# Block 2's q and x turned by VectorE and transfers instead of by TensorE, in a fused attention and SwiGLU kernel

## The chip, the cores and the metric

The kernel runs on one core of a Trainium2 chip. The metric is device time in microseconds (us) of that core. The kernel before took 1032.19 us, the median of three runs (1030.74 to 1032.48). A profile of one execution (1033.15 us, span 1031.2 us) stands behind every line below.

Names used: TensorE (PE in the profile, its weight loads PEld), VectorE (DVE), ScalarE (ACT), GpSimd (POOL), SyncE (SP, which computes nothing here but issues most transfers). SPq and ACTq are the instruction streams in which SP and ScalarE issue transfers.

## The reference, cut to what matters

```python
kv  = einsum('bhsd,bhse->bhde', k, v)          # batch 8, heads 8, seq 576, head_dim 64
a   = einsum('bhsd,bhde->bhse', q, kv)
a   = a / sqrt(mean(a*a, -1) + 1e-6) * g_norm
x   = a.transpose(0,2,1,3).reshape(4608, 512)  # tokens x model
g   = x @ w_gate                               # 512 x 1536
out = (g * sigmoid(g) * (x @ w_val)) @ w_out   # 1536 x 512
```

All is float32 for the purposes of this text. There is no softmax: attention is linear, so per head only the 64x64 matrix kv is needed.

## The kernel before, in words

**Blocks.** The 4608 tokens are worked in nine blocks of 512 (`BLK`), numbered 0 to 8. A block's attention (class `Att`) is woven into the feed-forward part (class `Ffn`) of the block before it: while block n is multiplied, block n+1's q is turned, multiplied by kv, scaled and turned again into x, with the model dimension on the partitions.

**Matrix products.** Block 0 is multiplied plainly (`plain_up`). From block 1 on the products are done in seven instead of eight block products (a Strassen-Winograd scheme; `Quad`, with numbers p = 1 to 7). Block 1 does this in one level for the up-projection (`Up`), blocks from `DEEP` = 2 on in two levels (`Inner`). The two-level form needs sums of weight blocks, called leaves here. They are computed once, during block 1, on VectorE (`leaf_steps`), are sent to DRAM by SP (tiles `w`, the helper `send`, L821), and are streamed back as 256 KB tiles `t` in every block from 2 on (class `Stream`, L793, 17 tiles for each third of the up-projection, through nine buffers). The pieces of work of a step are handed on: `Ffn.make` takes leaf steps in between matrix products; those of the last two weight pairs (j = 4 and 5) are kept in `latest` and are taken in the down-projection of block 1, in a room of 21 blocks named `xi`.

**Turning q and x.** There are two ways. In the first, TensorE multiplies by the identity, 16 products of 128x128 for q (`turn_q`, L335) and 16 for x (`turn_x`, L402), and a copy brings the result out of PSUM. In the second, q is loaded in strips of 32 columns (`load_quarters`, L281, 32 small transfers for a block), VectorE turns it in 32x32 blocks (L329), and no TensorE work is needed. For x, `blocks_x` turns 32x32 blocks on VectorE (L412), `place_x` puts the blocks into their places by 16 transfers (L426, eight on SP's queue and eight on ScalarE's), and `gain_x` multiplies by the gain in place (L431). The constant `TURNED` = 3 says from which block the second way is used; block 1's q (not its x) uses the strips as well. Block 2 uses the first way for both.

**The down-projection** (`Ffn.down`) runs the seven products in the order 1, 5, 6, 7, 2, 4, 3, or 1, 6, 5, 7, 2, 4, 3 where the next block is of the second way. After some of them a step of the next block's attention is put in (`Att.steps`): for the second way the whole attention after p = 1, the placing transfers after 5, the gain and the Strassen sums (`sums`) after 2. For the first way: half the attention after p = 1, x's first half and the second half of the attention after 6, x's second half and the sums after 2. `turn_t` lets GpSimd make three differences of `wo` tiles for each of p = 5, 7 and 4.

**What sets the order.** The statements are reordered engine by engine by a scheduler, whose priorities follow the program, and `tc.issue_after(x)` puts what is recorded within it behind x. Each engine then runs its own list in order, and a queue issues its transfers in order. The transfers of all queues share eight semaphores in turn: each waits for the one eight before it. In the built kernel before, SP's list in the down-projection of block 1 is: 20 of block 3's 32 q transfers, two leaf sends, the other 12, three weight tiles of block 2, two leaf sends, six more weight tiles, the two stores of block 1's output.

Of the kernel before, what the change touches and what calls it, by code (L numbers as in the profile page):

```python
# [14 lines left out]
P = 128  # L15
# [3 lines left out]
def kernel(  # L19
# [50 lines left out]
    NB = NT // BLK  # L70
# [44 lines left out]
    def ring():  # L115

        return r_pool.tile([P, 4, BLK], F32, name="r")
# [75 lines left out]
    class Att:  # L193


        def __init__(self, n):
            self.n = n

            self.cut, half = divmod(n, 2)
            self.split = half * D  # L200
            self.ps, self.z = {}, None
            self.q, self.k, self.v, self.room = [], {}, {}, None
            self.halves = []
            self.quarters = n == 1 or n >= TURNED

        def parts(self, t):

# [210 lines left out]
        def place_x(self):  # L418
            src = self.turned.rearrange("p i (x c) -> p (i x) c", c=P)
            self.x = x_pool.tile([P, 7, 2, HB], F32, name="x")  # L420
            dst = self.x[:, 0:4].rearrange("p o k (t c) -> p (o k t) c", c=P)
            rows = [slice(32 * r, 32 * (r + 1)) for r in range(4)]
            for a in range(4):
                for b in range(4):
                    queue = nc.scalar if b % 2 else nc.sync
                    queue.dma_start(out=dst[rows[b], :, rows[a]], in_=src[rows[a], :, rows[b]])  # L426

        def gain_x(self):
            for i in range(2):
# [56 lines left out]
        def steps(self):  # L486


            def whole():
                self.product(0, (m_psum, a_psum))  # L490
                self.product(1, (m_psum, b_psum))
                self.root(0, 2)
                for i in range(2):
                    self.scale(i)
                self.halves.append(self.scaled)
                self.blocks_x()

            def end():
                self.gain_x()
                self.sums()  # L500

            if self.n >= TURNED:
                return {1: whole, 5: self.place_x, 2: end}

            def last():
                self.turn_x(1)
                if self.n:
                    self.sums()

            def middle():  # L510
                self.turn_x(0)
                self.half(1, (m_psum, b_psum))


            return {1: lambda: self.half(0, (m_psum, a_psum)), 6: middle, 2: last}
# [7 lines left out]

    DEEP = 2

    TURNED = 3

    class Quad:

# [41 lines left out]
    class Up(Quad):  # L571
# [51 lines left out]
        def multiply(self, p):  # L623
            super().multiply(p)
            ffn = self.ffn
            if ffn.n != DEEP - 1:
                return

            if p == 5:
                self.leaf_room = ring().rearrange("p f (s c) -> p (f s) c", c=P)  # L630
            if p in (5, 7, 4):
                at = 3 * (5, 7, 4).index(p)
                ffn.making.extend(leaf_steps(self.j, [(self.w[p].unsqueeze(1), (p,))], self.leaf_room[:, at:]))
            if p == 3:
                if ffn.leaf_room is None:
                    ffn.leaf_room = x_pool.tile([P, 3, 7, P], F32, name="xi").rearrange("p a b c -> p (a b) c")
                halves = lambda t: t[self.j].rearrange("p (o i) c -> p o i c", o=2)
                steps = leaf_steps(self.j, [(halves(wg), (1, 2)), (halves(wv), (6, 3))], ffn.leaf_room)
                if self.j < NP - 2:
                    ffn.later.extend(steps)  # L640
                else:
                    ffn.latest.append(steps)

# [169 lines left out]
    def leaf_steps(j, sources, room):  # L813


        d, f = divmod(j, 2)
        i = 0

        def send(leaf, count, src):
            at = LEAVES.index(leaf)  # L820
            tc.keep_in_program_order(nc.sync.dma_start(out=stream.dram[d][:, at : at + count, f], in_=src))  # L821

        for t, os in sources:
            n = len(os)
            t = t.rearrange("p o i (e c) -> p o i e c", e=2)
            b11, t2_, b22 = t[:, :, 0, 0], t[:, :, 0, 1], t[:, :, 1, 1]
            to = room[:, i : i + 3 * n].rearrange("p (o r) c -> p o r c", r=3)
            yield lambda b22=b22, t2_=t2_: sub(nc.vector, t2_, b22, t2_)
            yield lambda b11=b11, t2_=t2_: add(nc.vector, t2_, t2_, b11)
            yield lambda t=t, t2_=t2_, to=to, n=n: sub(  # L830
                nc.vector, to[:, :, 0:3:2], t[:, :, 1], t2_.unsqueeze(2).to_broadcast([P, n, 2, P])
            )
            if os[0] not in RESIDENT:
                yield lambda t=t, o=os[0]: send((o, 1), 4, t[:, 0].rearrange("p i e c -> p (i e) c"))
            yield lambda b11=b11, t2_=t2_, to=to: sub(nc.vector, to[:, :, 1], b11, t2_)
            yield lambda i=i, n=n, o=os[0]: send((o, 4), 3 * n, room[:, i : i + 3 * n])
            i += 3 * n
# [88 lines left out]
    class Ffn:  # L926
# [52 lines left out]
        def down(self, nxt):  # L979

            down = self.down_
            fill = nxt.steps() if nxt else {}
            for p in (1, 6, 5, 7, 2, 4, 3) if 5 in fill else (1, 5, 6, 7, 2, 4, 3):
                if p == 1:
                    down.turn_t(7, self.ended)
                if p == 6:
                    down.turn_t(4, nxt.halves[0] if nxt and nxt.n >= TURNED else None)

                with tc.issue_after(nxt.multiplied.ins) if self.n == 0 and p in (5, 6) else ExitStack():
                    down.multiply(p)  # L990
                self.make(12)
                if p == 5 and self.n == DEEP - 1:
                    for i in range(2):
                        self.loads(i)
                if p in fill:
                    fill[p]()
                if p in (1, 7) and self.latest:

                    with tc.issue_after(nxt.scaled.ins):
                        for step in self.latest.pop(0):  # L1000
                            step()
                if p == 1:

                    with tc.issue_after(nxt.q_turned.ins) if self.n == 0 else ExitStack():
                        down.turn_s3()
# [60 lines left out]
    for n in range(NB):  # L1066
        ffn = Ffn(n, blocks[n])
        nxt = blocks[n + 1] if n + 1 < NB else None
        if n == 0:

            with tc.issue_after(squared.ins), tc.issue_after(scaled.ins):
                weights(2)
            ffn.plain_up(0, (0,))
            copied = blocks[0].copied
            blocks[0].turn_x(1)
            for f in range(NF):
                with tc.issue_after(blocks[0].copied.ins if f else copied.ins):
                    weights(2 * (f + 2))
                ffn.plain_up(f) if f else ffn.plain_up(0, (1,))
            weights(len(pieces))  # L1080
            pairs = wo.rearrange("p (j e) d -> p e j d", e=2)
            t2(pairs[:, 0, :, HD:DM], pairs[:, 1, :, HD:DM], pairs[:, 0, :, 0:HD])
            nxt.room = x_pool.tile([P, 3, 7, P], F32, name="xi").rearrange("p a b c -> p (a b c)")

            with tc.issue_after(sent.ins):
                for i in range(2):
                    nxt.load_kv(i)
                for i in range(2):
                    nxt.load_q(i)
            ffn.plain_end()  # L1090
            for g in range(2):
                nxt.kv(g)
        else:

            def third():
                nxt.kv(0)
                nxt.load_kv(1)

            def two_thirds():
                nxt.kv(1)  # L1100
                if nxt.n < TURNED:
                    for i in range(2):
                        nxt.load_q(i)

            ffn.up({4: third, 8: two_thirds} if nxt else {})
        if nxt:
            nxt.turn()
        if 0 < n < NB - 2:
            blocks[n + 2].load_kv(0)
        if TURNED - 2 <= n < NB - 2:  # L1110
            ffn.loads = blocks[n + 2].load_q
            if n >= DEEP:
                for i in range(2):
                    ffn.loads(i)
        ffn.down(nxt)
        if n == 0:
            blocks[2].load_kv(0)

            with tc.issue_after(nxt.halves[0].ins):
                for j in range(NP):  # L1120
                    t2(wv[j][:, 0:2], wv[j][:, 2:4], wg[j][:, 0:2])
# [31 lines left out]
```

## Time and profile before

| what | value |
|---|---|
| time, median of 3 | 1032.19 us |
| span of the profile | 1031.2 us |
| TensorE busy | 1013.0 us (98%) |
| VectorE busy | 703.9 us (68%) |
| GpSimd busy | 371.6 us (36%) |
| ScalarE busy | 230.2 us (22%) |
| HBM read, written | 138.02 MB, 22.41 MB |
| down-projection of block 1 (first product to block 2's start) | 238.6 to 279.8 us |
| same of block 2 (to block 3's start) | about 347.4 to 388.0 us |

How to read it: a line of the timeline has the start in us from the span's beginning, the duration, the engine, the line of the kernel, the operation with its tiles (out<-in) and how many were merged (x16). A bracket at the end tells how long the engine stood idle before it and what ended the wait. In the chain that ended last, the columns are start, duration and what. DVE x L111 and the like are the helpers `add`, `sub` and `mul` (L111 to L113). Matrix instructions come in two passes for each product of the program, so 12 products show as x24.

### The profile page before, as it was taken

The page shows a single profiled execution, that of the slowest core. Times are in us where ns is not written, and L with a number is a line of the kernel's source. Part 1 is how long each engine was busy: PE and PEld are TensorE (multiplying, and loading weights), DVE is VectorE, ACT ScalarE, POOL GpSimd, SP SyncE. Part 2 cuts the span into 40 slices and gives each one's busy share as a digit, 9 for nine tenths or more (in the row PEclk, how much of TensorE's full clock was granted, in tenths as well). Part 3 has the DMA queues.
Part 4 walks back from the last instruction along what each step waited for, and adds up shares of the span by engine and source line. Part 5 has one row for each costly group of instructions (what it writes and reads, how often), then busy time and mean ns, then how long its engine had stood idle before and what let it go on. Part 6 is the DMA issues. An engine that isn't in the chain of part 4 may idle for free.

```text
span 1031.2 us, 21440 instructions
## 1 busy us (share of the span) xinstructions
PE 1013.0 (98%) x8570; PEld 903.5 (88%) x8570; DVE 703.9 (68%) x1185; ACT 230.2 (22%) x359; POOL 371.6 (36%) x280
## 2 busy tenths in 40 slices
PE   5999999999999999999999999999999999999998
PEld 4544688888899989998999899988999899989997
DVE  2999796997766855585657576674669466856661
ACT  2666111222211211221112122111212111211110
POOL 0000543444035612462156305630455136513670
PEclk9999999999999999999999999999999999999999
DMA  7689614783778456855686468736862666066611
GB/s 215 195 261 266 119 37 128 186 223 72 205 202 248 90 133 209 248 126 114 192 242 163 68 205 240 198 53 186 236 199 50 169 196 193 22 165 205 189 30 41
DMA packets 252403, 168.15 MB, mean 163 GB/s; under 512 B 129168, under 2 KB 220432, under 8 KB 252304
## 3 DMA queue, kind: packets, MB, share of 16 engines
q1 hardware_dynamic: 225808, 163.37, 57.9%
q10 hardware_dynamic: 26432, 3.41, 2.0%
q8 instruction: 68, 1.11, 0.5%
q14 instruction: 31, 0.25, 0.1%
q0 software_dynamic: 64, 0.00, 0.0%
HBM read 138.02 MB, written 22.41 MB: 156 GB/s over the span
## 4 chain that ended last, share of the span: by engine, by line
PE 83%; DVE 10%; DMA 4%; SPq 1%; ACT 1%; issue 1%; DVEq 0%; ACTq 0%
PE b L712 26%; PE b L549 20%; PE c L712 13%; PE c L549 10%; PE a L712 6%; PE a L549 5%; DVE r L153 2%; PE m L355 1%; PE m L314 1%; SPq L281 1%; DVE r L147 1%; DMA h<-in_v_dram 1%; DVE r L152 1%; DMA ld<-in_v_dram 1%; DVE xi L112 1%
## 5 line engine op out<-in xcount | busy, mean ns | idle before, releaser
L111 POOL TENSOR_TENSOR r<-r 128x256 f32<-128x256 f32 (+1 forms) x105 | 110.7, 1060 | 310.1 <-DVE r L111 204.4
L111 DVE TENSOR_TENSOR r<-b,r 128x512 f32<-128x512 f32 (+1 forms) x273 | 162.1, 606 | 64.2 <-PE b L712 59.1
L112 POOL TENSOR_TENSOR t<-wo 128x512 f32<-128x512 f32 x81 | 117.1, 1470 | 191.6 <-DVE wo L111 106.9
L111 DVE TENSOR_TENSOR r<-c,r 128x512 f32<-128x512 f32 (+1 forms) x179 | 108.5, 618 | 95.0 <-PE c L712 55.5
L712 PE MATMUL b<-x,t 128*128 128x128 f32 x1092 | 151.0, 275 | 0.0
L712 PEld LDWEIGHTS b<-x,t 128*128 128x128 f32 x1092 | 136.5, 192 | 0.6
L111 DVE TENSOR_TENSOR r<-a,r 128x512 f32<-128x512 f32 (+1 forms) x99 | 62.5, 631 | 108.7 <-PE a L549 63.0
L712 PE MATMUL c<-xi,t 128*128 128x128 f32 x840 | 112.2, 275 | 0.4 <-DVE xi L111 0.4
L113 POOL TENSOR_TENSOR h<-r 128x1024 f32<-128x1024 f32 (+1 forms) x40 | 82.1, 2067 | 80.6 <-DVE r L111 72.8
L712 PEld LDWEIGHTS c<-xi,t 128*128 128x128 f32 x840 | 102.8, 192 | 0.5 <-DVE xi L111 0.5
L549 PE MATMUL b<-wo,h 128*128 128x256 f32 x432 | 99.5, 382 | 0.1
L549 PE MATMUL b<-t,h 128*128 128x256 f32 x432 | 96.9, 381 | 0.0
L549 PEld LDWEIGHTS b<-t,h 128*128 128x128 f32 x432 | 81.3, 190 | 11.3 <-issue 0.2
L549 PEld LDWEIGHTS b<-wo,h 128*128 128x128 f32 x432 | 79.9, 190 | 12.8 <-DVE h L113 2.5
L726 ACT COPY r<-b 128x512 f32<-128x512 f32 x63 | 36.9, 585 | 211.7 <-PE b L712 199.8
L712 PE MATMUL b<-xi,t 128*128 128x128 f32 x588 | 79.7, 276 | 0.0
L712 PEld LDWEIGHTS b<-xi,t 128*128 128x128 f32 x588 | 72.4, 192 | 0.0
L712 PE MATMUL b<-x,wg 128*128 128x128 f32 x336 | 52.7, 279 | 0.2 <-DVE x L112 0.2
L712 PE MATMUL b<-x,wv 128*128 128x128 f32 x336 | 51.3, 275 | 0.0
L549 PE MATMUL c<-t,s 128*128 128x256 f32 x216 | 48.3, 380 | 0.0
L549 PE MATMUL a<-wo,h 128*128 128x256 f32 x216 | 48.3, 379 | 0.0
L549 PE MATMUL c<-wo,h 128*128 128x256 f32 x216 | 48.1, 379 | 0.0
(131 smaller groups left out, 1579.8 us busy)
## 6 DMA issues: line engine op xcount, KB each, us to landing
t<-w SPq DMA_DIRECT2D x336, 256.0 KB, 3.6
out_dram<-r SPq DMA_DIRECT2D x17, 512.0 KB, 3.1
ld<-in_k_dram SPq DMA_DIRECT2D x26, 288.0 KB, 5.1
ld<-in_v_dram SPq DMA_DIRECT2D x26, 288.0 KB, 5.7
ld<-in_moe_w_gate_dram SPq DMA_DIRECT2D x12, 512.0 KB, 4.6
ld<-in_moe_w_val_dram SPq DMA_DIRECT2D x12, 512.0 KB, 4.4
ld<-in_moe_w_out_dram SPq DMA_DIRECT2D x12, 512.0 KB, 5.3
w<-t SPq DMA_DIRECT2D x18, 256.0 KB, 2.5
```

The lines of the kernel that those rows point to most:

```text
L111: add = lambda e, o, a, b: e.tensor_tensor(out=o, in0=a, in1=b, op=OP.add)
L112: sub = lambda e, o, a, b: e.tensor_tensor(out=o, in0=a, in1=b, op=OP.subtract)
L113: mul = lambda e, o, a, b: e.tensor_tensor(out=o, in0=a, in1=b, op=OP.mult)
L147: nc.vector.tensor_scalar(out=mag.bitcast(F32), in0=mag.bitcast(F32), scalar1=self.LOW, scalar2=self.HIGH, op0=OP.max, op1=OP.min,)
L152: nc.vector.tensor_scalar(out=sign, in0=high, scalar1=0x80000000, scalar2=None, op0=OP.bitwise_and)
L153: return nc.vector.scalar_tensor_tensor(out=mag, in0=mag, scalar=3, in1=sign, op0=OP.logical_shift_left, op1=OP.bitwise_xor)
L281: nc.sync.dma_start(out=to[32 * r : 32 * (r + 1), j, g0:g1], in_=q[b, 4 * i + 2 * j + h, s0 : s0 + 32 * (g1 - g0), 32 * d : 32 * (d + 1)]. ...
L314: nc.tensor.matmul(self.kv_ps[r][u * D : (u + 1) * D, g, :], lhsT=k[:, u, c, :], rhs=v[:, u, c, :], start=(c == 0), stop=(c == KT - 1),)
L355: self.multiplied = nc.tensor.matmul(self.ps[i][u][p : p + D, t, j, :], lhsT=self.qt[rows, 2 * i + t, j, p : p + D], rhs=kvs[b % 3][rows, ...
L549: nc.tensor.matmul(banks[e][:, e], lhsT=lhsT, rhs=rhs, start=first and i == 0 and (e == 0 or banks[0] is not banks[1]), stop=i == self.ste ...
L712: nc.tensor.matmul(ps[:, i, f], lhsT=self.weight(o, p, f), rhs=self.operand(o, p), start=first and (i, f) == (0, 0), stop=True, skip_group ...
L726: nc.scalar.copy(out=dst, in_=ps)
```

## The change

Block 2 goes over to the second way for both q and x, by `TURNED` = 2. Then the 32 products that turn them fall away from TensorE. Since the leaves of the last two weight pairs are still being made in that down-projection, they are moved: they now stand after p = 5 and p = 7, behind the scaling of block 2's attention and behind the last placing transfer of SP's queue (`nxt.placed`, a new name for it). Pair 5 gets a room of its own from the ring of work tiles instead of the second use of `xi`. The loads of block 3's q (`self.loads`) are put behind the same two marks. Which function builds the leaves' steps is now decided when their room is known (`steps` became a function of the room).

```diff
-            self.quarters = n == 1 or n >= TURNED
+            self.quarters = n > 0
...
-                    queue.dma_start(out=dst[rows[b], :, rows[a]], in_=src[rows[a], :, rows[b]])
+                    placed = queue.dma_start(out=dst[rows[b], :, rows[a]], in_=src[rows[a], :, rows[b]])
+                    if b % 2 == 0:
+                        self.placed = placed
...
-    TURNED = 3
+    TURNED = 2
...
-                steps = leaf_steps(self.j, [(halves(wg), (1, 2)), (halves(wv), (6, 3))], ffn.leaf_room)
+                steps = lambda room: leaf_steps(self.j, [(halves(wg), (1, 2)), (halves(wv), (6, 3))], room)
                 if self.j < NP - 2:
-                    ffn.later.extend(steps)
+                    ffn.later.extend(steps(ffn.leaf_room))
...
-                if p == 5 and self.n == DEEP - 1:
-                    for i in range(2):
-                        self.loads(i)
                 if p in fill:
                     fill[p]()
-                if p in (1, 7) and self.latest:
-
-                    with tc.issue_after(nxt.scaled.ins):
-                        for step in self.latest.pop(0):
+                if p in (5, 7) and self.n == DEEP - 1:
+
+                    with tc.issue_after(nxt.scaled.ins), tc.issue_after(nxt.placed.ins):
+                        room = self.leaf_room if p == 5 else ring().rearrange("p f (s c) -> p (f s) c", c=P)
+                        for step in self.latest.pop(0)(room):
                             step()
+                        if p == 5:
+                            for i in range(2):
+                                self.loads(i)
```

## The prediction

> **What bounds the kernel now.** I read the busy times first, then the chain that ended last, then the SP queue (which issues most transfers) around the place that the change touches: the down-projection of block 1, in which block 2's attention is worked out.
>
> ```profile
> PE 1013.0 (98%) x8570; PEld 903.5 (88%) x8570; DVE 703.9 (68%) x1185; ACT 230.2 (22%) x359; POOL 371.6 (36%) x280
> PE 83%; DVE 10%; DMA 4%; SPq 1%; ACT 1%; issue 1%; DVEq 0%; ACTq 0%
> ```
>
> TensorE is busy for 98% of the span and is 83% of the chain. Whatever leaves TensorE is won, as long as no other engine or transfer then comes too late for it. The chain in order of time shows what the change removes (columns: start, duration, what):
>
> ```profile
> 233.24 0.44 PE m L335 x4
> 233.67 0.22 PE b L335 x2
> ...
> 237.69 0.22 PE b L335 x2
> 237.91 0.44 PE m L335 x4
> 238.35 0.44 PE b L335 x4
> ...
> 255.62 0.87 PE m L402 x8
> ...
> 268.59 0.87 PE m L402 x8
> ...
> 279.82 0.89 PE b L712 x8
> ```
>
> L335 turns block 2's q, L402 its x; at 279.82 block 2's up-projection begins, with no pause before it. The SP queue in the same stretch:
>
> ```profile
> 238.73 10.36 SPq L281 DMA_DIRECT2D ld<-in_q_dram  x20
> ...
> 257.38 6.72 SPq L281 DMA_DIRECT2D ld<-in_q_dram  x12
> 264.21 1.40 SPq L793 DMA_DIRECT2D t<-w  x3
> ...
> 268.13 6.91 SPq L793 DMA_DIRECT2D t<-w  x6
> 275.29 5.68 SPq L936 DMA_DIRECT2D out_dram<-r  x2
> ```
>
> Block 3's q (L281) is asked for first, and then the first nine weight tiles of block 2 (L793). All nine are issued by 275.0, almost 5 us before block 2 starts. That is the slack which the change uses up. Block 2's own down-projection already does for block 3 what the change now does for block 2, so it has the prices:
>
> ```profile
> 344.15 17.80 SPq L281 DMA_DIRECT2D ld<-in_q_dram  x32
> 367.11 7.84 SPq L426 DMA_DIRECT2D x<-r  x8
> 375.07 3.44 SPq L793 DMA_DIRECT2D t<-w  x6
> ```
>
> There q goes out first, then x's placing transfers (L426), then the weight tiles. Last, one place where weight tiles are asked for late, at the start of block 6:
>
> ```profile
> 706.88 0.41 SPq L936 DMA_DIRECT2D out_dram<-r  x1
> 707.40 4.96 SPq L793 DMA_DIRECT2D t<-w  x9
> ```
> ```profile
> 713.82 0.71 PE L712 MATMUL a<-x,t 128*128 128x128 f32 x4 [0.79 <-DMA t<-w]
> ```
>
> The third of those tiles is released to TensorE at 713.77 in the chain, 6.9 us after the queue began this run with a store: 1.31 MB moved (0.52 of the store, three tiles of 0.26).
>
> [...] block 3's x needs two turns of 128x1024 (2.36 us together) and then 16 placing transfers. [...] So what stands behind a waiting transfer in SP's queue waits too; the trace agrees, SP issued nothing for 5.09 us at L426, waiting for VectorE. [...]
>
> **The change, part by part.**
>
> *Removed from TensorE.* q's turning takes 0.76 us at 233.24 to 234.00 and 1.10 us at 237.69 to 238.79: 1.86. x's takes 2 x 0.87 = 1.74. The two products (L355) stand apart now, 243.97 to 245.06 and 256.49 to 258.03, 2.63 us; block 3's in one piece took 353.84 to 355.86, 2.0 us: 0.6 less. Sum 4.2 us.
>
> *q in 32-wide quarters.* 32 small transfers in place of 4, at 0.53 us each on SP (17.0 to 17.8 us for 32 in all blocks), during block 1's up-projection, between the sends of weight leaves (L821). In the built order 16 of them come in a row behind the send that now starts at 213.4, so the sends that started at 215.2 move to about 222. Who waits: the leaf steps on VectorE that need their room again. VectorE meets the next such wait at about 227.7 (the instructions ahead of it summed), when the send of 222.9 should have landed (its median is 3.9 us). Bounds: 0, or up to 3 us if it lands late and TensorE then waits for VectorE. I take 0: both turns of q (2 x 1.23 against a copy of 0.69) fall at 230 to 233, where VectorE had 1.0 and 0.55 us idle.
>
> *x by VectorE and transfers.* Block 2's down-projection shows it: products at 353.84, x's transfers from 367.1 (13.3 us later), gain at 377.3, sums from 379.8, block 3 begins at 387.97 without a wait. Block 1 adds the leaves of the last two weight pairs to VectorE. Most fall into its 9.84 us idle before 376.89; the last 2.06 us stand ahead of x's sums. The sums TensorE needs third would be done some 2 us before their need. I price this at 0; at most 2 us.
>
> *The order on SP, the main point.* In the built order of the changed kernel SP has: two weight tiles, x's 8 transfers, two leaf sends, block 3's 32 q transfers, two more leaf sends, the store of block 1, and only then weight tiles three to nine. The waits on x's transfers and scaling were meant for the leaves, but q's loads stand behind the same ones, and the tiles behind q. Worked out:
> - Products start at 243.97 - 1.86, about 242.0. x's transfers from 242.0 + 13.2 = 255.2.
> - Eight of them on SP: 7.84 us in block 2, 5.76 in block 5; I take 7.4: 262.6.
> - Two leaf sends of 384 KB: 1.4 (1.32 and 1.76 before): 264.0. 32 q transfers: 17.4: 281.4.
> - The rest from block 6: 6.9 us for 1.31 MB. Here two sends, the store and tile three are 1.57 MB; the further 0.26 MB at about 290 GB/s (the rate of the stretch 215 to 225) adds 0.9. The tile lands at about 289.1; the tile behind costs TensorE 0.3 more: 289.4.
>
> When did the kernel before have as much done? The built order puts 20 of block 2's matrix products (two passes of 0.112 us each: 4.5 us) and 36 small k-v products (1.2 us) ahead of the first use of tile three: 279.8 + 4.5 + 1.2 = 285.5. From there both have the same work left. So the change costs 289.4 - 285.5 = 3.9 us. TensorE would arrive at about 281.3 and stand idle for near 8 us: the 4.2 us won are lost, and as much again. Later tiles follow at 0.9 us each, while TensorE takes some 1.4 us per tile (17 in a third of the up-projection, 23.3 us), so no second wait. 1032.2 + 3.9 = 1036.1; I say 1036.
>
> **Rivals.**
> - *All is hidden, faster.* If tile three landed by 281, only the 4.2 us of TensorE would count: 1028. For it: in blocks 2 to 7 the same scheme runs with no idle TensorE. Against: there q is loaded before x's transfers, and SP cannot bring 17 us of q, 7 of x and the sends between 255 and 281.
> - *Near balance.* Shorter x transfers (5.8), quick sends and a tile 5 us after its issue give a landing of about 286: 1032.5, no change that can be measured.
> - *More waits than one.* Leaf rooms late in the up-projection hold VectorE, by up to 3 us; SP's whole series then starts later by as much, so it adds fully: 1039. With slow transfers of x and q and longer landings: up to 1042.
>
> **How the numbers follow.** The late tile as worked out (1034.3 to 1039): 0.58. More waits (above): 0.17. Balance (1030.2 to 1034.2): 0.17. All hidden: 0.08. So slower 0.75, same 0.17, faster 0.08. SP's terms can err by 2 us down (x's transfers 1.6, sends 0.4) and by 3 up, and the waits of the up-projection only lengthen: 1031.5 to 1042 leaves out the hidden case and a little on both ends.
>
> **What would show it.** Right: SP shows L281 x32 between about 264 and 282, the tiles after it, and TensorE idle some 8 us before a use of t near 281 to 289, released by a DMA. L335 falls to the turns of block 0 and L402 to blocks 0 and 1. The start of block 2 at 275 to 276 confirms the gain. Wrong: block 2 entered later than 277 (x or VectorE is the bound), idle TensorE in 210 to 240 (leaf rooms), or the tiles issued before 278.

## The result, and the profile after

The changed kernel takes 1036.13 us, the median of four runs (1035.91 to 1037.1); the kernel before 1031.71 us in its four (1030.74 to 1032.48). The ratio is 1.0045, with a 95% interval of 1.0028 to 1.0063: slower by 4.4 us.

Busy times and the engines' shares of the chain, from the page of the changed kernel:

```profile
PE 1011.2 (98%) x8538; PEld 902.1 (87%) x8538; DVE 703.8 (68%) x1177; ACT 228.4 (22%) x354; POOL 371.4 (36%) x280
PE 87%; DVE 6%; DMA 3%; SPq 2%; issue 1%; ACT 1%; ACTq 0%; DVEq 0%
```

TensorE has 32 instructions fewer, 8538 against 8570 (a turning product is one pass, not two), and is busy for 1.8 us less, in a span that is 3.2 us longer. The queue of SP in the down-projection of block 1, in the timeline:

```profile
252.44 6.43 SPq L426 DMA_DIRECT2D x<-r  x8
259.89 0.97 SPq L823 DMA_DIRECT2D w<-xi  x2
261.00 18.37 SPq L281 DMA_DIRECT2D ld<-in_q_dram  x32
279.46 0.99 SPq L823 DMA_DIRECT2D w<-r  x2
280.55 1.64 SPq L938 DMA_DIRECT2D out_dram<-r  x1
282.29 4.37 SPq L795 DMA_DIRECT2D t<-w  x7
```

All 32 of block 3's q transfers (L281) now stand between x's placing transfers (L426) and all but the first two weight tiles of block 2 (L795). Tile three is the first of those seven, issued at 282.29. On TensorE, in the timeline:

```profile
263.33 0.79 PE L314 MATMUL m<-ld 64*64 64x64 f32 x34
...
269.34 5.34 PE L551 MATMUL c<-wo,h 128*128 128x256 f32 x24
274.52 0.61 PE L714 MATMUL b<-x,wg 128*128 128x128 f32 x4
...
279.18 0.81 PE L314 MATMUL m<-ld 64*64 64x64 f32 x38
286.65 1.23 PE L714 MATMUL a<-x,t 128*128 128x128 f32 x4 [6.67 <-DMA t<-w]
287.67 1.91 PE L714 MATMUL b<-xi,t 128*128 128x128 f32 x8
289.38 2.39 PE L714 MATMUL c<-xi,t 128*128 128x128 f32 x12
```

Block 2 begins at 274.52. TensorE then runs out at 279.98 and stands for 6.67 us until tile three lands. The chain, in order of time, holds the same transfer:

```profile
280.55 1.64 SPq L938
...
282.29 4.32 DMA t<-w
286.61 0.04 issue
286.65 1.23 PE a L714 x4
```

One thing more is to be seen in the timeline: the products behind the stop are slow. Eight products `b<-xi,t` take 1.91 us here, and 1.06 in the next use at 294.28. A table of stretches shows why (columns: stretch, its length, busy time of the five engines, granted TensorE clock, share of the DMA engines, GB/s):

```profile
283.00:284.00 1.00, 0.00 (x0) 0.00 (x0) 0.00 (x0) 0.00 (x0) 0.00 (x0) 1.00 1.05 376
284.00:284.50 0.50, 0.00 (x0) 0.00 (x0) 0.00 (x0) 0.00 (x0) 0.00 (x0) 0.90 1.07 279
284.50:285.00 0.50, 0.00 (x0) 0.00 (x0) 0.00 (x0) 0.00 (x0) 0.00 (x0) 0.50 0.93 209
...
290.50:291.00 0.50, 0.50 (x4) 0.50 (x4) 0.00 (x0) 0.00 (x0) 0.00 (x0) 0.50 0.99 381
291.00:291.50 0.50, 0.50 (x6) 0.50 (x5) 0.17 (x1) 0.00 (x0) 0.00 (x0) 0.77 1.06 410
```

The granted clock falls from 1.00 to 0.50 while TensorE stands and returns after it goes on. A mean of 0.90 over 284.0 to 284.5 puts the fall at 284.40, a mean of 0.77 over 291.0 to 291.5 the return at 291.23. From 286.65 to 291.23 TensorE worked at a granted clock of 0.50: 4.58 us for 2.3 us of work, as I estimate it (4.58 x 0.50). The 24 passes from 286.65 on took 4.95 us in all, against 2.68 before.

**The sum of it.** Two marks split the span: the product of block 1's up-projection after the one wait for VectorE, and the start of block 2. In the timeline of TensorE, before:

```profile
213.98 1.99 PE L549 MATMUL c<-x,wv 128*128 128x256 f32 x8 [0.74 <-DVE r L111]
...
279.66 0.61 PE L712 MATMUL b<-x,wg 128*128 128x128 f32 x4
```

After (block 2's start, at 274.52, is shown above):

```profile
212.43 1.99 PE L551 MATMUL c<-x,wv 128*128 128x256 f32 x8 [0.71 <-DVE r L111]
```

(The chain counts a start from the end of the product before it, so it has 279.82 for 279.66.)

| stretch | before | after | difference |
|---|---|---|---|
| start to the first mark | 213.98 | 212.43 | -1.55 |
| first mark to block 2's start | 65.68 | 62.09 | -3.59 |
| block 2's start to the end | 751.54 | 759.88 | +8.34 |

The first row I put down to single executions: in the profile of before the first loads landed 0.7 us later and TensorE waited 0.46 us at 124.33, neither in code that the change touches, and the second wait comes back in the profile of an experiment (0.34 us). The other rows are the change: 4.75 us lost between the first mark and the end, against 4.4 us by the medians. Of the 8.34 us, 6.67 are the stop and 2.3 the slow products behind it; 0.7 of k-v products of block 3 (L314, 34 passes at 263.33), which now lie ahead of block 2, go off. That leaves less than 0.1.

### The profile page after: what moved, and what is told of

The parts are those of the page before. It is cut to its first block, busy times and chain, and to the rows that moved or that the text cites. A ratio compares the mean times of both kernels' runs of the same rounds, so it can differ in the third digit from the quotient of the medians.

```text
span 1034.4 us, 21411 instructions
## 1 busy us (share of the span) xinstructions
PE 1011.2 (98%) x8538; PEld 902.1 (87%) x8538; DVE 703.8 (68%) x1177; ACT 228.4 (22%) x354; POOL 371.4 (36%) x280
## 4 chain that ended last, share of the span: by engine, by line
PE 87%; DVE 6%; DMA 3%; SPq 2%; issue 1%; ACT 1%; ACTq 0%; DVEq 0%
PE b L714 25%; PE b L551 19%; PE c L714 12%; PE c L551 9%; PE a L714 6%; PE a L551 5%; PE b L1021 4%; PE c L1021 4%; SPq L281 2%; PE m L314 1%; PE m L355 1%; DVE xi L112 1%; DMA t<-w 1%; DMA h<-in_v_dram 1%; DVE r L112 1%
```

## The experiments

Each ratio is to the kernel before, run on the same chip; 95% intervals in brackets.

**1. q early.** The loads go back to where they stood before the change, outside the two marks.

```diff
                 self.make(12)
+                if p == 5 and self.n == DEEP - 1:
+                    for i in range(2):
+                        self.loads(i)
                 if p in fill:
...
-                        if p == 5:
-                            for i in range(2):
-                                self.loads(i)
```

> The changed kernel with block 3's q loads taken out of the two marks and put directly after the product p = 5, as before the change; the queue then has them ahead of x's transfers. Late tile (my theory): the 6.67 us in which TensorE stood before its use of tile three fall away, and some 0.7 us of slowed products after it; 1028.5 us (1027.5 to 1029.5), 0.997 of the kernel before. TensorE enters block 2 without a stop for t. Rival, the work moved to VectorE costs (two turns of q, of x, leaves behind x): the place of a load does not matter to it, 1036. Rival, the bytes ahead of tile three (two sends, a store) and not the queue: the same bytes stand ahead of it here, so it stays at 1034 to 1036. Rival, x late: x's transfers now queue behind q, so x comes later and it gets worse, over 1037.

Measured: 1029.62 us, 0.9979 (0.997 to 0.9988). The stop for t is gone, and the VectorE and bytes rivals fall with it. It is 1 us short of the 1028.5 expected, and the trace shows where (queue of SP, then TensorE):

```profile
238.17 22.02 SPq L281 DMA_DIRECT2D ld<-in_q_dram  x32
260.30 6.07 SPq L426 DMA_DIRECT2D x<-r  x8
```
```profile
277.65 0.68 PE L714 MATMUL b<-x,wv 128*128 128x128 f32 x4 [0.95 <-DVE x L112]
...
281.63 0.68 PE L714 MATMUL b<-x,wg 128*128 128x128 f32 x4 [1.06 <-DVE x L112]
```

With all of q ahead, x's transfers start at 260.30 instead of 252.44, and TensorE waits some 2 us for x's sums on VectorE. The rival of a late x was right in its mechanism, and wrong in its size.

**2. Half of q early.** 16 transfers at the start of the down-projection, 16 left between x and the tiles.

```diff
             fill = nxt.steps() if nxt else {}
+            if self.n == DEEP - 1:
+                self.loads(0)
...
-                            for i in range(2):
-                                self.loads(i)
+                            self.loads(1)
```

> Half of block 3's q (16 transfers) goes early, the other 16 stay where the changed kernel has them, ahead of tiles two to nine. Late tile: the issue of tile three comes 9.2 us earlier, by about 273; it lands near 278, before its use at about 280, so the whole wait is gone: 1028.5 us, the same as with all of q early. If it lands 2 us later than that, 1029 to 1031. VectorE rival: 1036. Bytes rival: the store and sends still stand ahead: 1034 to 1036.

Measured: 1028.59 us, 0.9972 (0.9961 to 0.9983). The eight tiles behind q go out from 274.82 on, and the stop is gone. What is left of it in the first 35 us of block 2 is one short wait:

```profile
279.89 1.16 PE L714 MATMUL c<-xi,t 128*128 128x128 f32 x8 [0.21 <-DMA t<-w]
```

TensorE's longest wait in that stretch is 0.37 us, for VectorE.

**3. More of q.** 16 of the transfers are issued again, behind the 32 (`load_quarters` is made to take a tile that exists already).

```diff
...
                             for i in range(2):
                                 self.loads(i)
+                            blocks[3].load_quarters(0, blocks[3].q.pop(0))
+                            blocks[3].q.reverse()
```

> The changed kernel with 16 of block 3's q transfers issued a second time (the same data into the same place) behind the 32: a dose upward. Late tile: the tile comes 9 us later and all of it is seen, since TensorE already stands there: 1036.1 + 9 = 1045 us (1044 to 1046), with TensorE's stop for t at 15 to 16 us. VectorE rival: no change, 1036. Bytes rival: 0.5 MB more ahead of the tile at about 290 GB/s, 1.8 us: 1038.

Measured: 1044.27 us, 1.0124 (1.011 to 1.0138), 8.1 us above the changed kernel. The queue, and TensorE's stop:

```profile
261.52 26.40 SPq L281 DMA_DIRECT2D ld<-in_q_dram  x48
...
290.10 5.16 SPq L795 DMA_DIRECT2D t<-w  x7
```
```profile
294.87 1.22 PE L714 MATMUL a<-x,t 128*128 128x128 f32 x4 [14.47 <-DMA t<-w]
```

The 16 transfers took 8.0 us (26.40 less 18.37) and lengthened the stop by 7.8 (14.47 less 6.67): what stands in the queue ahead of the tile goes over into the time one for one. The bytes rival (1.8 us) is out.

**4. q split around the tiles.** The loads are written at the end of the down-projection; the built queue has 16 ahead of x's transfers and 16 behind the first nine tiles.

```diff
-                        if p == 5:
-                            for i in range(2):
-                                self.loads(i)
...
+            if self.n == DEEP - 1:
+                for i in range(2):
+                    self.loads(i)
```

> Block 3's q loads put at the end of the down-projection of block 1: the built queue has 16 of them ahead of x's transfers, and 16 behind the nine tiles and the last store. Late tile: tile three is asked for before 270, no stop at it; but the second 16 now stand ahead of tile ten, which is asked for at about 285 instead of 277: if it lands after its use (some 1.4 us per tile: tile ten is used near 290) there is a small stop there. 1028.5 us without, up to 1030 with. VectorE rival: 1036.

Measured: 1028.50 us, 0.9971 (0.996 to 0.9983). Queue of SP:

```profile
252.96 6.37 SPq L426 DMA_DIRECT2D x<-r  x8
...
271.07 3.83 SPq L795 DMA_DIRECT2D t<-w  x6
276.38 0.39 SPq L938 DMA_DIRECT2D out_dram<-r  x1
276.82 9.63 SPq L281 DMA_DIRECT2D ld<-in_q_dram  x16
286.56 8.61 SPq L795 DMA_DIRECT2D t<-w  x13
```

x starts where it did in the changed kernel, the first nine tiles are out by 275, and tile ten goes out at 286.56; no product up to 310 us is shown waiting for t. This is the change with its order mended, faster than both kernels.

**5 and 6. A small dose, for the clock.** Six and eight of the 32 transfers are sent ahead of x's, the rest stay. `load_quarters` is given a condition on its counters j and r; the diff is that of six, with eight the condition is `j == 0`.

```diff
+                if p == 5 and self.n == DEEP - 1:
+                    blocks[3].load_quarters(0, lambda j, r: r < 3 and j == 0)
...
-                            for i in range(2):
-                                self.loads(i)
+                            blocks[3].load_quarters(0, lambda j, r: not (r < 3 and j == 0))
+                            blocks[3].load_quarters(1)
```

> The changed kernel with 6 of block 3's 32 q transfers sent ahead of x's transfers, the other 26 where the changed kernel has them. A small dose, for the clock: in the changed kernel's trace TensorE's granted clock falls to 0.50 about 4.4 us after TensorE stops and is back 4.6 us after it goes on. Queue and clock: the tile comes 3.0 us earlier (0.50 us each), the stop falls from 6.7 to about 3.7 us, which ends before the clock falls, so another 1.8 us of slow products goes too: 1036.1 - 4.8 = 1031.3 us (1030.8 to 1032), clock 1.0. Queue alone, with the slow products due to something else (the next tiles, contention): 1033.1 us, products after the stop as slow as before.

> The same with 8 transfers ahead. Queue and clock: one more us off, 1030.3 us (1029.8 to 1031), stop about 2.7 us, clock 1.0. Queue alone: 1032.1.

Measured: 1033.83 us with six, 1.002 (1.0013 to 1.0028), and 1032.66 us with eight, 1.0009 (1.0001 to 1.0018). Both are between the changed kernel and the full gain, as the dose asks, but 2.5 us above what I expected with the clock: a shorter stop did not spare the clock (35 of the 36 runs of the two have a mean of 0.998 or less). They lie nearer to what was expected if the slow products had another cause (1033.1 and 1032.1), so these two medians do not tell that apart; experiment 9 does. The profile with eight has a stop of 2.45 us only:

```profile
282.13 0.71 PE L715 MATMUL a<-x,t 128*128 128x128 f32 x4 [2.45 <-DMA t<-w]
282.92 2.04 PE L715 MATMUL b<-xi,t 128*128 128x128 f32 x8
```
```profile
282.00:284.00 2.00, 1.80 (x9) 1.64 (x10) 1.01 (x2) 0.00 (x0) 0.00 (x0) 0.73 1.01 327
...
285.50:286.00 0.50, 0.50 (x4) 0.50 (x4) 0.26 (x1) 0.00 (x0) 0.00 (x0) 0.50 0.79 182
286.00:287.00 1.00, 1.00 (x10) 1.00 (x9) 0.40 (x1) 0.00 (x0) 0.00 (x0) 0.83 0.95 356
```

The clock fell at 282.92, when TensorE was already at work again, and was back at 286.34. TensorE had stood from 279.68, so the fall came 3.2 us after the stop began, where the changed kernel had 4.4. These two kernels also vary more from run to run than the others (1031.3 to 1036.6 with six, 1030.4 to 1034.6 with eight), and the clock varies with them. The mean granted clock of each run is on record; the profiled run with eight, with 3.42 us at 0.50, has 0.998. Of the 36 runs one has 1.000, 16 have 0.998 and 19 less, and those with less are the longer ones: 1034.5 us in the mean against 1032.7 with six, 1033.5 against 1031.6 with eight. How much of this is the clock itself, and how much a longer stop that brings a lower clock with it, the short runs don't tell.

With six, the profiled execution was the longest of 22, so it does not give the usual size of the stop, but it shows what varies. Counted from the first mark its tile three was issued 3.0 us earlier than in the changed kernel, as six transfers ask, but took 6.12 us to land instead of 4.32, so the stop was still 5.44 us; and of the 6.84 us at a clock of 0.50, 5.9 fell on work, where the changed kernel had 4.58. Why the landing varies is open.

**7. q alone.** The kernel before with only the strips for block 2's q.

```diff
-            self.quarters = n == 1 or n >= TURNED
+            self.quarters = n > 0
```

(and in the main loop the two conditions of the change that tell when q is loaded; `TURNED` stays 3)

> The kernel before with one part of the change: block 2's q in strips turned by VectorE, x still by TensorE, leaves and block 3's q loads as before. By the sum of the prediction TensorE loses 1.86 us, and nothing waits: 1031.8 - 1.9 = 1029.9 us. VectorE or leaf rooms late in the up-projection: not faster, 1031.8 or more.

Measured: 1028.80 us, 0.9975 (0.9965 to 0.9985).

**8. x alone.** The fourth experiment with block 2's q left to TensorE.

```diff
-            self.quarters = n > 0
+            self.quarters = n == 1 or n >= 3
```

> The other part alone: block 2's x by VectorE and transfers with the leaves behind x, block 2's q by TensorE as before; block 3's q loads split as in the fourth experiment, so that no tile is late. By the sum TensorE loses 1.74 us of turning and 0.6 us of split products: 1031.8 - 2.3 = 1029.5 us. If x or its sums come late (VectorE), 1030.5 to 1032.

Measured: 1028.96 us, 0.9973 (0.9961 to 0.9984).

Each part alone is faster than before, so neither the work moved to VectorE nor the rooms of the leaves cost what TensorE wins. From the first mark to block 2's start the traces have 63.72 us with q alone, 64.05 with x alone, 62.30 with both (experiment 4) and 65.68 before. With x alone and with both, the 34 k-v passes (0.7 us) lie in this stretch too, and have to be taken out: 2.0 us won by q, 2.3 by x, 4.1 by both. The parts add up within 0.2 us, and the prediction had 1.86, 2.3 and 4.2.

The medians show as much or a little more for the parts (2.6 and 2.4 us), and less for both (3.3). The trace of experiment 4 shows a loss behind the mark: from 287.61 to 292.31 TensorE takes 4.70 us for 24 passes that took 2.68 before and 38 k-v passes worth 0.8, so 1.2 us go in short waits. 0.25 of these are for VectorE; the cause of the rest is not shown. So 1028.5 need not be the best that this change can give.

**9. TensorE kept busy.** The changed kernel, with seven products more whose results nothing reads.

```diff
             for i, o in enumerate(self.outers):
+                if (self.ffn.n, self.d, o, p) == (2, 0, 5, 2):
+                    self.ffn.warm()
...
+        def warm(self):
+            ps = m_psum.tile([P, NS, P], F32, name="m")
+            for _ in range(7):
+                nc.tensor.matmul(ps, lhsT=ident, rhs=wo[:, 0], start=True, stop=True)
```

> The changed kernel with seven extra products of 128x512 on TensorE (0.87 us each, two ahead of block 2 and five ahead of the stop), whose results nothing reads. The tile is asked for by a queue that does not look at TensorE, so it lands when it did; TensorE is busy for 6.1 of the 6.7 us in which it stood. Clock: the granted clock does not fall, [...] and the 1.7 us of slow products behind the stop go: 1036.1 - 1.7 = 1034.4 us (1033.9 to 1035), though TensorE has 6.1 us more to do; stop 0.6 us. Slow products from contention or from the next tiles instead: they stay slow, 1036.1 us. Work that really bounds (TensorE and not the tile): plus 6.1, 1042 us.

Measured: 1034.41 us, 1.0031 (1.0019 to 1.0043). TensorE in the timeline:

```profile
277.80 4.46 PE L953 MATMUL m<-wo,ident 128*128 128x512 f32 x10
...
285.86 0.71 PE L716 MATMUL a<-x,t 128*128 128x128 f32 x4 [1.06 <-DMA t<-w]
286.70 1.13 PE L716 MATMUL b<-xi,t 128*128 128x128 f32 x8
287.90 1.58 PE L716 MATMUL c<-xi,t 128*128 128x128 f32 x12
```

With 6 us more to do the kernel is 1.7 us faster than the changed one (1.4 by the two ratios, whose intervals overlap). The traces settle it: counted from the first mark, the tile lets TensorE go on at the same moment (74.22 us in the changed kernel, 74.20 here), and the same 24 passes behind it are over after 3.45 us instead of 4.95. The clock stays at 1.00 in the trace (the mean is 1.000 in all six runs, 0.994 to 0.997 in the changed kernel's four), although the DMA engines are as busy with the next tiles as there (a share of 1.02 over 286 to 292, against 0.97). So 1.5 of the 2.3 us were the clock and not contention; the other 0.8 (3.45 us for 24 passes that take 2.68 without a wait) remain at full clock. That extra work costs nothing shows once more that the tile sets the time.

## Why the prediction was right

The mechanism was the one named: the loads of block 3's q, drawn behind x's two marks, hold back the weight tiles on SP's queue. Experiments 1, 2 and 4 take them away in three ways, and the stop goes each time; experiment 3 adds to them, and the stop grows by as much.

- *4.2 us leave TensorE.* Right: 3.59 us by the marks, and 0.7 of k-v products that moved into the stretch besides, so 4.3. L335 is gone from block 1, L402 from its down-projection, and the products in one piece take 2.09 us where the two pieces took 2.77.
- *q's strips priced at 0 in the up-projection.* Right: TensorE's one wait there is 0.71 us (0.74 before), and VectorE's turns fit in.
- *x by VectorE priced at 0.* Right: block 2 starts without a wait for x.
- *SP's series.* From the products (240.39) to x's transfers 12.0 us, not 13.2. The eight took 6.43 (7.4 taken), the sends 0.97 (1.4), q 18.37 (17.4). Between the eight and the sends SP waited 1.0 us for a transfer of x to land, for which the sum had nothing. From the next send to the landing of tile three 7.15 (7.8). Single terms were off by up to 1.2 us in both directions; together the tile came about 1 us earlier than said, counted from the same mark.
- *The stop.* 6.67 us, not the 8.1 between 281.3 and 289.4. Counted from the first mark TensorE went on 1.2 us earlier than said (the tile 0.9, and the 0.3 for the tile behind it did not show) and arrived 0.2 later.
- *What was missing: slow products behind the stop.* The sum had TensorE at full speed there. It lost 2.3 us, 1.5 of them to the clock by experiment 9.

That the number fits so well is in part luck. The sum had 8.1 us of stop; measured are 6.67 of stop and 2.3 of slow products, 9.0 together. A stop that was too long hid most of what was missing, and the change is 4.4 us by the medians where the sum had 3.9. And the sum started from 1032.2 us, while the median of the kernel before over four runs is 1031.71: these 0.5 us bring 1036.1 and 1036.13 together.

The rival "all is hidden" gave 1028 for the case that the tile comes in time; with the order mended it is 1028.5.

## What to carry to other kernels

Before putting transfers behind a wait, read what follows them on the same queue: here everything behind inherited it, and 32 small transfers of 0.57 us each made a wall of 18.37. To see what a queue entry costs, add and take away some of them; a slope of one says that it stands on the path. And where a tuned engine is made to stand, count its slow restart with the stop: here 2.3 us behind 6.67.

## What the runs showed of the hardware

How long the granted clock was 0.50, from the stretches of each trace: 3.42 us (stop 2.45, experiment 6), 6.83 (stop 6.67, the changed kernel), 6.84 (stop 5.44, experiment 5, 285.96 to 292.80) and 13.65 (stop 14.47, experiment 3, 284.87 to 298.52). The three longer ones are 2.0, 2.0 and 4.0 times the shortest; why, these traces do not show. In experiment 6 the fall came 3.2 us after the stop began, with TensorE at work again; in the other three it came 4.4 to 4.5 us after, within the stop. A stop of 1.06 us (experiment 9) left the clock at 1.00.
